# A table of due times in place of a seeded search, for a kernel whose order is packed ahead of the run

## The chip, the core and the metric

The kernel runs on one core of a Trainium2 chip. Its time is the device time of one launch in microseconds (us), the median of several runs. TensorE is called PE here, VectorE DVE, ScalarE ACT, GpSimd POOL, and the engine that issues the DMAs SP.

## What is computed

The program has two parts. The first is a linear attention with a delta rule: 4 batches of 8 heads, 768 steps, head width 48. The second is a gated layer over all 3072 tokens, with 384 features in, 1536 hidden and 384 out (called the expert layer or MoE here).

```python
k_n = k / (np.linalg.norm(k, axis=-1, keepdims=True) + 1e-06)
for t in range(S):
    kt, vt, bt = (k_n[:, :, t], v[:, :, t], beta[:, :, t, None])
    y[:, :, t] = np.einsum('bhd,bhde->bhe', q[:, :, t], state)
    v_old = np.einsum('bhde,bhd->bhe', state, kt)
    state = state + bt[:, :, :, None] * np.einsum('bhd,bhe->bhde', kt, vt - v_old)
...
a = x @ w_a
b = x @ w_b
return (a * b @ w_out).astype(np.float32)
```

Here `x` is the attention's output `y`, with the heads side by side.

## The kernel before, in words

**Tiling and stages.** The 768 steps are cut into 24 chunks of 32 steps, in six groups of four. For each group there is a stage `prep` (norms of the keys, products of keys and queries within a chunk, with 64 small products per chunk), a stage `solve` (a triangular system for each chunk, worked on DVE as a long chain of pairs of multiply into `tmp` and subtract from `b`), and a stage `steps` (for each chunk: products with the state `sh`, a difference `f`, a product with the solved factors `tt`, the update of the state `S_ps` from `u`, the output product with `at`, and then norm, transpose and split of y into two f16 halves `xb`). The small products of attention use 32- or 64-row tiles of the PE array; those of a chunk come as one operation, a group of 32 calls. In groups 2 to 5 POOL multiplies the values `vnb` with the norms; in groups 0 and 1 DVE does.

The expert layer works on pairs of chunks (256 tokens) and on 12 slices of 128 hidden features. For a pair and a slice there are two operations of 9 full products (`xb` by the weights `wh`, into a bank), then ACT scales one into `a`, DVE multiplies into `g`, ACT and DVE split `g` into the f16 halves `ghl`, and two operations of 3 products with `wo` add to the output. The stages `w0` to `w11` load, decode and scale one slice of weights each. The tile `late` holds several things in turn: weights as loaded, pieces of later chunks, and outputs.

**The order.** The kernel isn't issued in the order in which it is written. Each call on an engine is recorded as an operation of a `Plan` (`add`); calls inside `plan.group()` on one engine become one operation. There are 2937: 790 on PE, 1214 on DVE, 640 on ACT, 154 on POOL with its short copies, and the DMAs on SP. `link` finds the dependencies from the regions that are read and written. `pack` then runs through the work with a price for each operation, a list of those that are ready on each engine, and a due time `pri` for each: at each step an engine that is free takes its ready operation with the lowest due time, unless a rule holds it back (a bank of PSUM that isn't free, a `hold` time, small tiles that are preferred to full ones for a while after small ones, `JOIN`; an instruction fetch). The result is one sequence of operations, the bank that each uses (`bind`), and how many filler products of the tile `ones` PE gets ahead of an operation in the first part (`fill`). `issue` then emits the instructions in that sequence, and on the chip each engine takes its own instructions strictly in the order of emission, waiting on semaphores.

```python
while wait[e] and wait[e][0][0] <= t:
    i = heapq.heappop(wait[e])[1]
    heapq.heappush(can[e], (pri[i], i))
i = None
while can[e] and i is None:
    i = heapq.heappop(can[e])[1]
```

In the kernel before, `order` gets its due times in two steps. Fifteen passes of `pack`, forwards and backwards, set an operation's due time from how late it may end, less a fixed boost for its stream (`boost`), with the first loads ahead of everything. Then 30 fixed seeds each change some due times in `jitter`: 3% of the operations, or one stream, or 200 operations in a row, by random amounts. The last `pack` makes the sequence. All of this happens before the launch and isn't part of the measured time.

Of the kernel before, what the change touches and what calls it, by code (L numbers as in the profile page):

```python
# [40 lines left out]
def boost(o):  # L41
    return BOOST.get(o.stream + ("_pe" if o.stream == "moe" and o.eng == "PE" else ""), 0.0)
# [19 lines left out]
        self.rd, self.wr, self.deps, self.tag, self.banks = {}, {}, set(), "", set()  # L62


def jitter(pri, ops, seed):
    r = random.Random(seed)
    kind, amp = r.randrange(3), r.choice((500.0, 3000.0, 10000.0, 30000.0))
    names = sorted({o.stream for o in ops})
    name, start = r.choice(names), r.randrange(len(ops))
    move, new = r.gauss(0.0, amp), []  # L70
    for i, (o, p) in enumerate(zip(ops, pri)):
        u, g = r.random(), r.gauss(0.0, amp)
        if o.stream != "load":
            if kind == 0 and u < 0.03:
                p += g
            elif kind == 1 and o.stream == name:
                p += move
            elif kind == 2 and start <= i < start + 200:
                p += g
        new.append(p)  # L80
    return new


class Plan:
# [391 lines left out]
    HOLD = 300.0  # L476
    MARGIN = 5000.0
    WINDOW = 3413.0
    PASS = 15
    SEEDS = (500003, 500005, 500019, 500020, 500026, 500028, 500084, 500091, 500108, 500109, 500111, 500120, 500124, 500177, 500284, 500305, 500553, 500626, 500636, 500644, 500735, 500743, 500761, 500845, 500953, 501051, 501128, 501296, 501447, 501757)  # L480

    def order(self):


        self.link()
        ops = self.ops
        self.first = {o.eng: o for o in reversed(ops)}
        self.users = {}
        for o in ops:
            for b in o.banks:  # L490
                self.users[b] = self.users.get(b, 0) + 1
        self.succ = [[] for _ in ops]
        self.pred = [[] for _ in ops]
        for i, o in enumerate(ops):
            for j in o.deps:
                late = self.late(ops[j], o)
                self.succ[j].append((i, late))
                self.pred[i].append((j, late))
        pri = [o.pri - boost(o) - 1e12 * (o.stream == "load") for o in ops]
        for _ in range(self.PASS):  # L500
            found = self.pack(pri)
            stop = found[1] if found else [float(k) for k in range(len(ops))]
            _, stop, _, total, _ = self.pack([-t for t in stop], True)
            pri = [k - 1e12 if o.stream == "load" else total - t - boost(o) for k, (o, t) in enumerate(zip(ops, stop))]
        for seed in self.SEEDS:
            pri = jitter(pri, ops, seed)
        best = self.pack(pri)
        self.bind, self.fill = best[4]
        return best[2]

# [766 lines left out]
```

## Time and profile before

| what | value |
|---|---|
| runs | 632.46, 634.51, 637.12 us; median 634.51 |
| profiled execution | 633.64 us; its span from first to last instruction 631.9 us |
| PE busy | 608.3 us, 96% of the span |
| DVE, ACT, POOL busy | 435.6, 287.7, 56.5 us |
| granted PE clock, mean | 0.989 |
| moved by DMA | 42.85 MB |

How to read it: busy is the time in which an engine had an instruction under way, and since PE's instructions overlap, a busy PE isn't PE at its peak. A row of a group of instructions has the line of the code, engine, operation, output and inputs by the program's names, shape and count, then busy us, mean ns of one, the idle time of the engine just before them and what ended it. "issue" is time in which the engine waited for nothing that the profile shows. Since all instructions are emitted by `issue`, nearly all have one line, L532, and the filler has L523; tiles are told apart by name. A `bank` is a bank of PSUM, whatever it holds. Products of f32 show as two instructions each, so an operation of 32 small products shows as 64.

### The profile page before, as it was taken

The numbers are of one execution on the slowest core, as the hardware profiler recorded it, in microseconds if no ns is written. First come the engines' busy times: TensorE is split into PE (matmuls) and PEld (weight loads), VectorE is DVE, ScalarE is ACT, GpSimd is POOL, SyncE is SP. The second block draws the span as 40 slices with busy tenths as digits, with TensorE's granted clock in tenths as the row PEclk, the third lists the DMA queues.
The fourth block names the chain that finished last, engine by engine and source line by source line (L and its number), as shares of the span: only waits on it lengthen the run. The fifth ranks groups of instructions, "written<-read, shape, count | busy, mean of one in ns | idle before, by whom it ended". The sixth has DMA issues, their size and how long they took to land.

```text
span 631.9 us, 27357 instructions
## 1 busy us (share of the span) xinstructions
PE 608.3 (96%) x12228; PEld 476.9 (75%) x12228; DVE 435.6 (69%) x1215; ACT 287.7 (46%) x773; POOL 56.5 (9%) x158
## 2 busy tenths in 40 slices
PE   7989999999999998999999999999999999999997
PEld 6855767677778786777877787777878788787885
DVE  4977998889976789469965468875598544542222
ACT  2067863565843332544354334364423534542332
POOL 0221210110102102000020000020000000000000
PEclk8969999999999999999999999999999999999999
DMA  8554551352046510023200023100000000000000
GB/s 315 177 163 122 144 138 39 97 134 79 30 121 196 153 52 2 3 63 120 85 27 21 21 89 107 35 28 4 4 3 26 2 15 16 4 26 1 13 13 25
DMA packets 20756, 42.85 MB, mean 68 GB/s; under 512 B 2208, under 2 KB 5280, under 8 KB 20640
## 3 DMA queue, kind: packets, MB, share of 16 engines
q1 hardware_dynamic: 20640, 41.12, 21.7%
q8 instruction: 95, 1.56, 1.0%
q14 instruction: 21, 0.17, 0.1%
HBM read 36.39 MB, written 4.72 MB: 65 GB/s over the span
## 4 chain that ended last, share of the span: by engine, by line
PE 75%; DVE 11%; DMA 6%; issue 3%; ACT 3%; POOL 1%; SPq 0%; DVEq 0%; POOLq 0%; ACTq 0%
PE bank L532 73%; DMA late<-in_w 4%; PE S_ps L532 2%; DVE late L532 1%; DVE wh L532 1%; DVE b L532 1%; DVE g L532 1%; DMA rawb<-in_kqt 1%; DMA wh<-in_w 1%; DVE ghl L532 1%; DVE tmp L532 1%; DVE f L532 1%; DMA vnb<-in_vn 1%; DVE y L532 1%; POOL late L532 0%
## 5 line engine op out<-in xcount | busy, mean ns | idle before, releaser
L532 PEld LDWEIGHTS <-wh 128*128 128x128 f16 x2592 | 250.2, 98 | 46.4 <-issue 5.2
L532 PE MATMUL bank<-xb,wh 128*128 128x256 f16 x2160 | 257.5, 273 | 3.3 <-issue 2.0
L532 PE MATMUL bank<-wo,ghl 128*128 128x384 f16 x864 | 163.0, 326 | 1.8 <-issue 0.7
L532 ACT ACTIVATE a<-bank,part 128x256 f32<-128x256 f32 x144 | 68.0, 473 | 161.4 <-PE bank L532 159.9
L532 DVE TENSOR_TENSOR g<-bank,a 128x256 f32<-128x256 f32 x144 | 60.6, 422 | 84.7 <-ACT a L532 82.9
L532 PEld LDWEIGHTS <-ghl 128*128 128x128 f16 x864 | 81.4, 98 | 46.4 <-issue 1.9
L532 ACT CAST ghl<-g 128x256 f16<-128x256 f32 x144 | 58.0, 404 | 67.7 <-DVE g L532 50.5
L532 DVE TENSOR_TENSOR ghl<-g,ghl 128x256 f16<-128x256 f32 x144 | 61.0, 425 | 33.6 <-ACT ghl L532 30.2
L532 DVE TENSOR_TENSOR tmp<-b,b 128x31 f32<-128x31 f32 (+20 forms) x154 | 50.3, 327 | 3.1
L532 DVE TENSOR_TENSOR b<-b,tmp 128x31 f32<-128x31 f32 (+20 forms) x154 | 49.7, 322 | 3.5
L532 PE MATMUL bank<-late,wh 128*128 128x256 f16 x432 | 51.1, 273 | 0.0
L532 ACT ACTIVATE ys<-y 128x96 bf16<-128x96 f32 x96 | 26.1, 273 | 10.0 <-DVE y L532 9.7
L532 PE MATMUL bank<-rawb 48*32 48x64 f32 x1280 | 22.6, 220 | 7.0 <-POOL late L532 2.4
L532 PEld LDWEIGHTS bank<-rawb 48*32 48x32 f32 x1280 | 19.4, 108 | 10.6 <-POOL late L532 2.9
L532 POOL TENSOR_TENSOR z<-z,kb 128x4 f32<-128x4 f32 x24 | 9.6, 400 | 197.2 <-DVE z L532 181.6
L532 DVE TENSOR_TENSOR f<-vnb,bank 128x384 f32<-128x384 f32 x38 | 19.6, 548 | 8.7 <-PE bank L532 8.7
L532 ACT COPY sh<-S_ps 112x768 f32<-112x768 f32 x23 | 18.3, 796 | 14.6 <-PE S_ps L532 14.6
L532 PEld LDWEIGHTS bank<-sh,rawb 48*64 48x64 f32 x1216 | 19.9, 134 | 5.2 <-issue 2.1
L523 PE MATMUL bank<-ones 128*128 128x256 f32 x78 | 22.2, 450 | 1.1 <-DVE ones L532 1.1
L532 PE MATMUL bank<-sh,rawb 48*64 48x48 f32 x1216 | 22.5, 220 | 0.1
L532 PE MATMUL bank<-u,at 32*32 32x48 f32 x1536 | 21.5, 203 | 0.6 <-issue 0.6
L532 DVE SCALAR_TENSOR_TENSOR y<-bank,kb,y 128x384 f32<-128x384 f32 x23 | 14.2, 616 | 11.4 <-ACT y L532 10.4
(127 smaller groups left out, 640.8 us busy)
## 6 DMA issues: line engine op xcount, KB each, us to landing
late<-in_w SPq DMA_DIRECT2D x40, 288.0 KB, 3.2
rawb<-in_kqt SPq DMA_DIRECT2D x32, 256.0 KB, 2.7
out<-late SPq DMA_DIRECT2D x24, 192.0 KB, 1.9
vnb<-in_vn SPq DMA_DIRECT2D x10, 384.0 KB, 3.6
kb<-in_kn SPq DMA_DIRECT2D x9, 384.0 KB, 3.6
wh<-in_w SPq DMA_DIRECT2D x8, 288.0 KB, 3.3
rawb<-in_kqt SPq DMA_DIRECT2D x2, 1024.0 KB, 7.2
late<-in_kqt SPq DMA_DIRECT2D x8, 256.0 KB, 2.6
```

The source lines that it names most:

```text
L523: self.nc.tensor.matmul(self.pool[-1][0 : 32 + 96 * k, 0 : 32 + 224 * k], one, one.unsqueeze(1).broadcast_to([P, 1 + k, 32 + 96 * k])[:, 0 ...
L532: fn(*(self.place(a, lease) for a in args), **{k: self.place(a, lease) for k, a in kw.items()})
```

## The change

`jitter`, `PASS`, `SEEDS` and the passes are gone. In their place stands a table `DUE` of 2937 whole numbers, one for each operation in the order in which the program records them; ten times a number is the operation's due time, and `pack` runs once with these. Values near -99999999999 belong to the first loads. Operations, prices, holds, leases and `pack` itself are as before.

```diff
-import random
...
-def jitter(pri, ops, seed):
-    r = random.Random(seed)
-    kind, amp = r.randrange(3), r.choice((500.0, 3000.0, 10000.0, 30000.0))
...
+DUE = (
+    -12125,-8933,-13218,-100000000000,-100000000000,-100000000000,-99999999999,-99999999999,-99999999999,-99999999999,-99999999999,-99999999999,
...
+    49978,51481,60596,61726,60332,60386,52777,52323,52862,53125,61737,60175,64048,61278,58533,52510,52971,48928,60557,52767,52460,49435,
+)
...
-    PASS = 15
-    SEEDS = (500003, 500005, 500019, 500020, 500026, 500028, 500084, ...
...
-        pri = [o.pri - boost(o) - 1e12 * (o.stream == "load") for o in ops]
-        for _ in range(self.PASS):
-            found = self.pack(pri)
-            stop = found[1] if found else [float(k) for k in range(len(ops))]
-            _, stop, _, total, _ = self.pack([-t for t in stop], True)
-            pri = [k - 1e12 if o.stream == "load" else total - t - boost(o) for k, (o, t) in enumerate(zip(ops, stop))]
-        for seed in self.SEEDS:
-            pri = jitter(pri, ops, seed)
-        best = self.pack(pri)
+        best = self.pack([10.0 * p for p in DUE])
```

More of the change, by code (lines that the diff above doesn't have):

```diff
@@ L62, in __init__ @@
         self.rd, self.wr, self.deps, self.tag, self.banks = {}, {}, set(), "", set()
-def jitter(pri, ops, seed):
-    r = random.Random(seed)
-    kind, amp = r.randrange(3), r.choice((500.0, 3000.0, 10000.0, 30000.0))
[L68 to L81, printed above, removed]
+DUE = (
[117 rows of a table added]
+)
 class Plan:
@@ L478 @@
     WINDOW = 3413.0
-    PASS = 15
-    SEEDS = (500003, 500005, 500019, 500020, 500026, 500028, 500084, 500091, 500108, 500109, 500111, 500120, 500124, 500177, 500284, 500305, 500553, 500626, 500636, 500644, 500735, 500743, 500761, 500845, 500953, 501051, 501128, 501296, 501447, 501757)
     def order(self):
```

115 rows, old and new, of the table DUE are left out of this document.

## The prediction

> **What bounds the kernel now.** I read the page first, then the windows of all engines, PE's waits, the groups by shape, and last the timeline at three places.
>
> ```profile
> span 631.9 us, 27357 instructions
> PE 608.3 (96%) x12228; PEld 476.9 (75%) x12228; DVE 435.6 (69%) x1215; ACT 287.7 (46%) x773; POOL 56.5 (9%) x158
> PE 75%; DVE 11%; DMA 6%; issue 3%; ACT 3%; POOL 1%; SPq 0%; DVEq 0%; POOLq 0%; ACTq 0%
> ```
>
> PE is busy for 608.3 of 631.9 us and makes three quarters of the chain that ended last. An order of work can't make a product shorter. It can only remove what PE loses: idle time, filler products, and the loss at each change between small and full tiles. So I look for these three, by stage. In the next rows the columns are the stretch, then busy us and count for PE, weight load, DVE, ACT and POOL, then PE's granted clock.
>
> ```profile
> 0.00:20.00 20.00, 16.83 (x292) 13.66 (x293) 11.49 (x28) 4.89 (x9) 2.03 (x12) 0.91 0.83 284
> 20.00:40.00 20.00, 17.64 (x310) 13.06 (x308) 18.90 (x47) 5.39 (x18) 5.10 (x12) 0.85 0.57 165
> 40.00:60.00 20.00, 17.53 (x650) 11.97 (x650) 13.95 (x43) 15.21 (x45) 2.99 (x9) 0.89 0.51 140
> 100.00:120.00 20.00, 19.90 (x325) 14.29 (x326) 19.03 (x50) 8.77 (x25) 0.95 (x3) 1.00 0.09 23
> 240.00:260.00 20.00, 17.95 (x426) 14.04 (x424) 13.49 (x38) 7.75 (x17) 3.42 (x4) 1.00 0.01 2
> 580.00:600.00 20.00, 20.00 (x167) 16.06 (x165) 5.53 (x13) 6.23 (x14) 0.00 (x0) 1.00 0.03 11
> 0.00:60.00 60.00, 51.99 (x1249) 38.69 (x1250) 44.34 (x116) 25.49 (x71) 10.12 (x32) 0.89 0.64 196
> 60.00:500.00 440.00, 428.32 (x9325) 336.87 (x9326) 343.95 (x976) 213.06 (x573) 44.94 (x122) 1.00 0.23 67
> 500.00:560.00 60.00, 60.00 (x1109) 47.55 (x1107) 27.22 (x77) 26.77 (x80) 1.41 (x4) 1.00 0.03 9
> 620.00:640.00 20.00, 8.02 (x59) 5.50 (x57) 2.37 (x6) 3.23 (x7) 0.00 (x0) 0.94 0.06 20
> ```
>
> Idle PE time stands in three places: 60.00 - 51.99 = 8.0 us up to 60 us, 440.00 - 428.32 = 11.7 us from 60 to 500 us, and 11.9 - 8.02 = 3.9 us in the tail. From 500 to 620 us PE has no gap. The tail is the last scaling and the output transfer, which no order shortens.
>
> ```profile
> L532 PE MATMUL bank<-xb,wh 128*128 128x256 f16 x2160 | 257.5, 273 | 3.3 <-issue 2.0 <-DVE z L532 0.5 <-DVE at L532 0.4
> L532 PE MATMUL bank<-wo,ghl 128*128 128x384 f16 x864 | 163.0, 326 | 1.8 <-issue 0.7 <-ACT sh L532 0.6 <-DVE z L532 0.5
> L523 PE MATMUL bank<-ones 128*128 128x256 f32 x78 | 22.2, 450 | 1.1 <-DVE ones L532 1.1
> L532 PE MATMUL bank<-late,wh 128*128 128x256 f16 x432 | 51.1, 273 | 0.0
> 66.92 1.15 PE L532 MATMUL bank<-xb,wh 128*128 128x256 f16 x9
> ```
>
> The second loss is the filler: 22.2 us of products of `ones`, which compute nothing. The first product of the expert layer (the MoE part of the program) starts at 66.92 us. That layer has 2160 + 432 + 864 = 3456 products. In 580 to 600 us, with nothing else, 167 of them take 20.00 us, 0.1198 us each, so all need 414 us. From 66.92 to the start of the tail at 628.0 us there are 561.1 us; minus 414 and 11.7 of gaps leaves 135 us for the attention's small products, the late weights, and the third loss, the change of tile shape.
>
> ```profile
> 351.43 1.15 PE L532 MATMUL bank<-late,wh 128*128 128x256 f16 x9
> 352.51 0.88 PE L532 MATMUL bank<-f,tt 32*32 32x48 f32 x64
> 353.60 1.10 PE L532 MATMUL bank<-late 48*32 48x64 f32 x64 [0.21 <-DVE g L532]
> 354.63 0.93 PE L532 MATMUL S_ps<-u,kb 32*48 32x48 f32 x64
> 355.50 2.14 PE L532 MATMUL bank<-late,wh 128*128 128x256 f16 x18
> 357.47 1.14 PE L532 MATMUL bank<-wo,ghl 128*128 128x384 f16 x6
> ```
>
> A stretch of small tiles (352.51 to 355.50 here) stands between full ones, and such stretches come again for every chunk. From 66.92 us on about 21 of the 24 chunks have their five groups of small products still ahead, at about 1.0 us a group (the mean of the 0.88, 1.10 and 0.93 here, an estimate for all five): 105 us. With 10 to 15 us for the side products and the late weights that is 115 to 120 us, and 15 to 20 of the 135 us are lost at changes of shape; I use 18 us.
>
> **The change part by part.** It removes `jitter`, the 15 passes and the 30 seeds, and gives each of the 2937 operations its own due time. Instructions, tiles, prices, holds and leases stay. It adds no wait by itself: the packing still starts the ready operation with the lowest due time and keeps every dependency. What moves is the place of an operation in its engine's queue. I compared the two lists of due times by rank alone. On PE half of the 790 operations move by at most 4 places, a tenth by more than 16. On DVE half of the 1214 move by more than 28. The largest shift by stage is in the DVE work of the triangular solves of groups 4 and 5, whose middle operations are due 97 and 127 places earlier. The 24 first loads keep their sequence up to one v load, two places earlier on SP; later weight and piece loads change by up to 8 places, in a queue whose DMA share is 0.03 to 0.23 after 60 us. I cost these DMAs at nothing; bounds from the DMA waits below are 1.8 us either way. What is left are three terms.
>
> ```profile
> PE bank L532 <- issue: 5.5, 10, 0.7
> PE bank L532 <- POOL late L532: 2.4, 2, 1.4
> PE bank L532 <- DMA rawb<-in_kqt: 1.8, 1, 1.8
> PE bank L532 <- POOL vnb L532: 1.6, 1, 1.6
> PE bank L532 <- DVE b L532: 1.2, 1, 1.2
> PE bank L532 <- ACT ys L532: 1.1, 1, 1.1
> PE bank L532 <- DVE zi L532: 1.1, 2, 0.7
> PE bank L532 <- DVE z L532: 1.1, 2, 0.5
> ```
>
> *Term 1, up to 66.92 us.* The chain is the load of the pieces, the solve of group 0 on DVE, the first two chunks, then the first product. DVE is 18.90 of 20 us busy in 20 to 40 us, so a cheaper place for it is scarce; in 40 to 60 us it is 13.95 busy and PE waits 1.1 us for ys and 1.1 us for zi. These 2.2 us are pure order: short operations queued behind weight decoding. Filler and gaps together (22.2 + 8.0 us) bound the gain, but before 30 us they cover DMA and the solve. I take -2.0 us, bounds -8.0 (all gaps) and +3.0 (the waits for ys, zi and b once more, 3.4 us, rounded down).
>
> *Term 2, gaps from 60 to 500 us.* Of 11.7 us the waits for operations that stand late in another queue are POOL late 2.4, POOL vnb 1.6, DVE z 1.1 and four smaller ones of ACT sh, ACT u, DVE at and DVE g of 1.4 together: 6.5 us. Most of the rest is issue time (5.5 us over the whole span), which a new order moves and doesn't remove. The two solves that come due earlier are also the ones that make later chunks, and so PE work, available. I take two thirds of 6.5, -4.5 us; bounds -10 and +6 (the 6.5 us of waits once more).
>
> *Term 3, changes of shape.* With the PE operations sorted by due time alone, small tiles stand in 91 stretches in the old list and 83 in the new one; the order that was issued has 85. 18 us over 85 is 0.21 us each, so 8 fewer are -1.7 us; bounds -5 (a quarter of 18, rounded) and +1.7.
>
> The sum: -2.0 - 4.5 - 1.7 = -8.2 us. The profiled execution took 633.64 us (its span 631.9 and 1.7 around it), so 625.4 us; the median of the runs, 634.51, is 0.9 higher, so 626.3. I say 626, which is 1.3% faster. About 1%, 6.3 us, is what a measurement of this kernel can tell from no change.
>
> One cover can go: the granted clock.
>
> ```profile
> 34.00:42.00 8.00, 7.29 (x231) 0.51 0.55 152
> ```
>
> In the rows above the clock is 0.91, 0.85 and 0.89 up to 60 us, and 1.00 after; inside, from 34 to 42 us, it is 0.51. If the lower state is one half, that is 2 x (0.09 + 0.15 + 0.11) x 20 = 14 us at half speed, mostly under filler and waits, worth at most 7 us. The longest wait of PE in the table is 1.8 us, and the clock stayed at 1.00 through all later ones, so I put no price on it. [...]
>
> **The rivals.**
>
> *Nothing to measure, 632 us.* The gaps change places. For it: in 100 to 120 us DVE is busy for 19.03 of 20 us and PE for 19.90, so what is moved forward on DVE there delays something else; the issue waits stay; only term 1 and a part of term 3 hold, together 2 to 3 us. It also covers the case that the table hardly does what it says, since dependencies, holds and bank leases may force nearly the old order. Against it: 6.5 us of gaps wait for an operation and not for an engine's capacity, and half of DVE's queue moves.
>
> *Slower, 641 us: the solves run beside POOL's products.* The place is the end of the solve of group 2, before's largest gap after 60 us:
>
> ```profile
> 238.37 0.40 DVE L532 TENSOR_TENSOR tmp<-b,b 128x231 f32<-128x231 f32 x1
> 238.57 3.90 POOL L532 TENSOR_TENSOR vnb<-vnb,nm 128x384 f32<-128x384 f32 x4 [16.53 <-DVE nm L532]
> 238.69 0.82 DVE L532 TENSOR_TENSOR s<-nm 128x32 f32<-128x32 f32 x1
> 241.83 0.86 DVE L532 TENSOR_TENSOR tmp<-b,b 128x207 f32<-128x207 f32 x1
> 243.13 1.10 PE L532 MATMUL bank<-rawb 48*32 48x64 f32 x64 [1.61 <-POOL vnb L532]
> 245.14 0.33 DVE L532 TENSOR_TENSOR tmp<-b,b 128x175 f32<-128x175 f32 x1
> ```
>
> While POOL multiplies, a DVE step takes 0.86 us for 207 elements, where 231 took 0.40 just before: each such step loses up to 0.46 us, and behind it wait the evictions that free PE's banks. PE lost 20.00 - 17.95 = 2.05 us in this window. Before has this meeting with such a loss once. If solves meet the v products of the three other groups of this kind too (the four groups after the first two use POOL for them), PE loses 3 x 2.05 = 6.2 us, at most 3 x 3.90 = 11.7 us when DVE stands still for all of POOL's time. With none of the gains that is 633.6 + 6.2 = 639.8, up to 645.3; I name 641. It decides when, in three groups, DVE's spare time in the 20 us around the meeting falls below the 3.90 us of POOL. Against it: in the latter half DVE has such time (13.49 busy of 20 here), and a solve with a due time earlier by 100 places may also come clear of the products. [...]
>
> *Much faster, 613 us.* Term 1 reaches its bound of -8.0, term 2 -8 and term 3 -4: 633.6 - 20 = 613.6. For it: filler and gaps of the start hold 30 us. Against it: DVE's 18.90 of 20 us there, and the loads.
>
> **How the numbers follow.** The forecast (616 to 628) has 0.46, much faster (under 616) 0.09, nothing to measure (628 to 638) 0.37, slower (over 638) 0.08. The line for faster by over 1% is 634.5 - 6.3 = 628.2, nearly the forecast's upper edge; I count 0.54 as faster, leaving 0.38 within 1% and 0.08 slower. The terms' bounds added up give 610.6 and 644; not all of them fall on one side at once. The range of 8 in 10 takes the forecast, the upper part of "nothing to measure" and a little of the third rival: 614 to 637.
>
> **What would show it.** Term 1: the first MoE product starts before 66.92 us, at about 65. Term 2: PE's idle time from 60 to 500 us is about 7 us instead of 11.7, without the two waits on POOL. Term 3: fewer stretches of small tiles, about 78. The tail stays near 3.9 us and PE has no gap from 500 us on. [...]

## The result, and the profile after

The changed kernel takes 629.44 us (median; 627.59 to 630.36), against 635.30 us (632.46 to 637.12) for the kernel before, each in 7 runs. The ratio is 0.9919, with a 95% interval from 0.9898 to 0.9940. So the table makes the kernel faster by 0.8%, 3.8 to 6.5 us, where 8.2 us were forecast. Of all runs below, one of 646.36 us lies over 1.5% above the fastest run of its kernel, and it is left out of that kernel's median. The profiled execution took 629.44 us, its span 627.7 us, 4.2 us shorter than before.

From the page of the changed kernel, the same lines as before and the line of the loads of instructions, which comes up again below:

```profile
span 627.7 us, 27362 instructions
...
PE 607.3 (97%) x12228; PEld 476.6 (76%) x12228; DVE 434.2 (69%) x1215; ACT 286.7 (46%) x773; POOL 57.1 (9%) x158
...
q8 instruction: 95, 1.56, 1.0%
```

The windows of the changed kernel (stretch, then busy us and count of PE, weight load, DVE, ACT, POOL, then PE's clock):

```profile
0.00:60.00 60.00, 51.34 (x1218) 38.78 (x1221) 44.16 (x116) 24.43 (x67) 8.63 (x32) 0.86 0.62 194
60.00:500.00 440.00, 431.78 (x9397) 339.50 (x9390) 342.75 (x977) 214.27 (x586) 46.59 (x122) 1.00 0.22 67
500.00:560.00 60.00, 60.00 (x1108) 47.43 (x1107) 27.61 (x76) 26.45 (x73) 1.86 (x4) 1.00 0.04 14
...
620.00:640.00 20.00, 4.17 (x26) 2.29 (x24) 1.38 (x4) 1.97 (x4) 0.00 (x0) 0.94 0.05 20
```

PE's idle time from 60 to 500 us fell from 11.7 to 440.00 - 431.78 = 8.2 us. Up to 60 us it rose a little, from 8.0 to 8.7 us. The tail is 7.7 - 4.17 = 3.5 us, before 3.9. Together the idle time is 3.2 us less, and PE's busy time is 1.0 us less (607.3 after 608.3): that is the 4.2 us.

PE's waits in the changed kernel (us in total, times, longest):

```profile
PE bank L623 <- issue: 4.6, 8, 1.1
PE bank L623 <- DVE g L623: 2.5, 5, 1.0
PE bank L623 <- DMA rawb<-in_kqt: 2.3, 1, 2.3
...
PE bank L623 <- ACT wh L623: 1.3, 1, 1.3
PE bank L623 <- DVE zi L623: 1.3, 2, 0.7
...
PE bank L623 <- DVE z L623: 1.0, 2, 0.5
```

The two rows on POOL, `late` with 2.4 us and `vnb` with 1.6 us before, are gone. In their place stand five waits on `g`, 2.5 us, where before had this row:

```profile
PE bank L532 <- DVE g L532: 0.2, 1, 0.2
```

How the wait on `vnb` went is seen in the timeline of the changed kernel, where the multiplications of group 3's values now come ahead of the group's first products:

```profile
223.84 1.78 POOL L623 TENSOR_TENSOR vnb<-vnb,nm 128x384 f32<-128x384 f32 x2 [4.53 <-DVE nm L623]
223.91 1.03 DVE L623 TENSOR_TENSOR tmp<-b,b 128x231 f32<-128x231 f32 x1
...
228.97 1.79 POOL L623 TENSOR_TENSOR vnb<-vnb,nm 128x384 f32<-128x384 f32 x2 [3.23 <-DMA vnb<-in_vn]
229.12 0.96 DVE L623 TENSOR_TENSOR tmp<-b,b 128x252 f32<-128x252 f32 x1
...
230.12 0.93 DVE L623 TENSOR_TENSOR b<-b,tmp 128x252 f32<-128x252 f32 x1
...
231.08 0.42 DVE L623 TENSOR_TENSOR tmp<-b,b 128x255 f32<-128x255 f32 x1
...
232.35 1.62 PE L623 MATMUL bank<-wo,ghl 128*128 128x384 f16 x9 [1.02 <-DVE g L623]
```

POOL's four multiplications still meet the solve on DVE, now in two pairs, 15 and 10 us earlier than the four in a row of before. One step beside the first pair takes 1.03 us, two beside the second 0.96 and 0.93 us, the next one 0.42. Behind the second pair `g` is late and PE waits 1.02 us, where it had lost 2.05 us between 240 and 260 us before.

The first product of the expert layer starts at 67.30 us, not earlier than the 66.92 of before:

```profile
67.30 0.93 PE L623 MATMUL bank<-xb,wh 128*128 128x256 f16 x7
```

### The profile page after: what moved, and what is told of

Same layout as the page of the kernel before. It is cut to its first block, busy times and chain, and to the rows that moved or that the text cites. A ratio compares the mean times of both kernels' runs of the same rounds, so it can differ in the third digit from the quotient of the medians.

```text
span 627.7 us, 27362 instructions
## 1 busy us (share of the span) xinstructions
PE 607.3 (97%) x12228; PEld 476.6 (76%) x12228; DVE 434.2 (69%) x1215; ACT 286.7 (46%) x773; POOL 57.1 (9%) x158
## 3 DMA queue, kind: packets, MB, share of 16 engines
q8 instruction: 95, 1.56, 1.0%
## 4 chain that ended last, share of the span: by engine, by line
PE 72%; DVE 11%; DMA 7%; issue 4%; ACT 3%; POOL 1%; SPq 0%; DVEq 0%; POOLq 0%; ACTq 0%
PE bank L623 70%; DMA late<-in_w 5%; PE S_ps L623 2%; DVE b L623 2%; DVE g L623 1%; DVE tmp L623 1%; DMA wh<-in_w 1%; DMA rawb<-in_kqt 1%; DVE ghl L623 1%; DVE wh L623 1%; DVE late L623 1%; POOL vnb L623 1%; DVE f L623 1%; DMA vnb<-in_vn 1%; ACT a L623 1%
```

## The experiments

My theory after the result was that the gain is made of PE waits removed one by one after 60 us. The rivals were that the start carries it; that a removed wait comes back later; and that it is a matter of where PE's instructions stand in their stream, since eight to ten waits ("issue") have no releaser in the profile.

For the experiments a kernel gets a finished sequence, the bank of every lease and the filler, in place of the table:

```diff
-        best = self.pack([10.0 * p for p in DUE])
-        self.bind, self.fill = best[4]
-        return best[2]
+        self.bind, self.fill = dict(enumerate(BIND)), FILL
+        return list(SEQ)
```

A mixture of two sequences takes the operations of one up to a point, and then all others in the other's order. Where a lease's bank is taken there, it gets another that is free. That touched 0 to 6 leases of 345 in the mixtures at one cut, and 11 and 27 in the two with an inserted stretch. Each run stands beside runs of the kernel before on the same chip, 633.7 to 634.8 us in the median.

### The start alone, and the rest alone

```diff
-SEQ = new
+SEQ = new up to 62 us, then old          (e1_new_start)
+SEQ = old up to 62 us, then new          (e2_old_start)
```

> The new sequence for what is planned up to 62 us, then the old one for the rest. Theory (the gain is waits of PE removed after 60 us): no gain, 0 to +0.6 us on before, so about 635 us where before is 635. Rival (the gain is in the start): 629 to 630 us.

> The old sequence for what is planned up to 62 us, then the new one for the rest. Theory: the whole gain of the change, 628.5 to 629.5 us where before is 635. Rival (the start): 634 to 635 us.

Measured: with the new start 634.20 us, ratio 0.9990 (0.9963 to 1.0018), no gain. With the old start and the new rest 629.22 us, ratio 0.9913 (0.9880 to 0.9946), the whole gain. The rival of the start falls, though the first interval leaves room for a part of up to 2.3 us.

### How the gain adds up

```diff
+SEQ = new up to 180 us, then old         (e3_new_to_180)
+SEQ = new up to 345 us, then old         (e9_new_to_345)
```

> The new sequence up to 180 us, then the old one. Theory (waits removed one by one along the span; the new kernel is 1.5 us ahead at the eighth chunk's norm): 1.5 us less than before, 633.5 where before is 635. Rival (all comes from the two waits on POOL at 243 and 327 us): as before, 635. Rival (start and the stage where DVE is full, 60 to 180 us, carry it): 630.

> The new sequence up to 345 us, then the old one. Theory (the gain adds up along the span from removed waits): about two thirds of the gain of 5 to 6 us, 630.5 to 632 where before is 634.5. Rival (the gain needs the whole of the new sequence, and a mixture loses it): as before, 634.5. Rival (all of it is won by 345 us): 629.

Measured: 633.57 us, ratio 0.9973 (0.9953 to 0.9993), then 630.53 us, ratio 0.9940 (0.9908 to 0.9973). After 180 us a third of the gain is there, after 345 us about three quarters. Both medians are what the theory said. The second interval doesn't exclude that all of the gain is won by 345 us, and neither run says which kind of loss shrinks.

### One stretch at a time

```diff
+SEQ = old, but the operations planned for 200 to 262 us in the new order   (e7_old_but_200_262)
+SEQ = old, but the operations planned for 300 to 345 us in the new order   (e8_old_but_300_345)
```

> The old sequence, with the operations of the stretch planned for 200 to 262 us put into the new sequence's order (58 places of PE and 107 of DVE differ; group 3's norms come earlier). Theory (a removed wait of PE is worth its length): the wait of 1.6 us on POOL and the 0.45 us behind it at 243 us go, a wait of about 1 us on g comes, as in after; 1 to 2 us less than before, 633.5. Rival (a removed gap comes back later, since the next chunk isn't earlier): as before, 635, with the idle time moved into the next 100 us.

> The old sequence, with the operations of the stretch planned for 300 to 345 us in the new order (32 places of PE, 64 of DVE). Theory: the wait of 1.35 us on POOL late at 327.6 us shrinks to 0.4 us as in after; about 1 us less than before, 634. Rival: as before, 635, with the time lost elsewhere.

Measured: 634.27 us, ratio 0.9994 (0.9970 to 1.0019), and 633.89 us, ratio 0.9996 (0.9968 to 1.0024). Neither gains a microsecond that can be told. In the first, the waits aimed at did change. Its waits of PE:

```profile
PE bank L591 <- issue: 8.3, 11, 1.4
...
PE bank L591 <- POOL late L591: 1.3, 1, 1.3
PE bank L591 <- DVE g L591: 1.2, 2, 1.0
...
PE bank L591 <- POOL vnb L591: 0.4, 1, 0.4
```

The wait on POOL vnb shrank from 1.6 to 0.4 us and one on g came, as in the changed kernel. But the issue waits grew from 5.5 to 8.3 us. In the second, the wait of 1.35 us on POOL at 327 us went, and at the same product an issue wait of 1.16 us stood in its place:

```profile
327.98 1.10 PE L591 MATMUL bank<-rawb 48*32 48x64 f32 x64 [1.16 <-issue]
```

A stretch's gain of 1 to 2 us is within the interval of these runs, so its size stays open. What the two traces show is that the issue waits aren't a fixed background: they move with the order, by as much as the waits on engines do.

### Where the instructions stand in PE's stream

`pack` itself counts PE's instructions. Its `fetch` takes them in blocks of 256, from a start of 63 (`BEGIN`), prices the load of each block and holds an operation back whose block would not have come; after 60 us it does the same for counts 14 lower and 14 higher (`SHIFTS`). So each order is built for its own place, and the shifts that follow are all larger than what it allows for.

The next runs leave the sequence alone and change the filler ahead of it, so that all later instructions of PE stand some places later or earlier.

```diff
-FILL = {60: [0, 7], 72: [0, 3], 122: [0, 28], 248: [0, 1]}
+FILL = {60: [0, 7], 72: [0, 3], 122: (64, 20), 248: [0, 1]}    (e4_after_shift, 96 later)
+FILL = {60: (32, 7), 72: [0, 3], 122: [0, 28], 248: [0, 1]}    (e5_after_shift64 and e6_before_shift64, 64 later)
```

The numbers are counts of small and large filler products ahead of an operation. A later variant puts one product of 512 columns in place of two of 256:

```diff
-FILL = {... 122: [0, 28] ...}
+FILL = {... 122: (0, 0, 14) ...}      (e10_after_wide14 and e11_before_wide14, 56 earlier)
+FILL = {... 122: (0, 14, 7) ...}      (e12_after_wide7, 28 earlier)
```

> The new sequence, but in the third stretch of filler 8 large products give way to 64 small ones, so 96 more instructions stand ahead of everything that follows on PE at nearly the same time. Theory (the gain is in the order): as after, within 1 us, 629 to 630.5. Rival (the gain is where PE's instruction stalls fall by chance, the issue waits): up to 3 us slower, 631 to 633, with other issue waits and more of them.

> The new sequence with all its filler, and 32 small products (64 instructions) more in the gap of 2.3 us ahead of PE's first real products, where PE waits for a DMA anyway; all that follows stands 64 instructions later in PE's stream. Theory A (the gain is in the order, and the place of the instructions in PE's stream matters little): 629 to 630 where before is 635. Rival B (the order is fitted to the places at which PE's instructions arrive): more issue waits than the 4.6 us of after, 2 to 5 us slower than after, 631 to 635.

> The same 32 small products ahead of the old sequence. Theory A: as before, 634 to 636. Rival B: if the old order is fitted as well, slower by as much as the run with the new order, 637 to 640; if the old one isn't fitted and the new one is, as before, and then the gain is that fit.

> The new sequence, with 14 filler products of double width in place of the 28 of the third stretch: same busy time on PE, 56 instructions fewer ahead of all the rest. Theory B (the order is fitted to the places at which PE's instructions arrive): slower than after by 3 to 8 us, 632 to 638, with more issue waits after 60 us. Theory A (the loss of the run with 64 instructions more came from the start alone): as after, 628.5 to 630.5.

> The same double-width filler ahead of the old sequence. Theory B: slower than before, 637 to 643, and slower than the same shift on the new order by 2 to 6 us, if the new order keeps a gain of its own at any place. Theory A: as before, 634.5. If it comes out equal to the new order with the same shift, the gain of the change is fit to the places and nothing else.

> The new sequence, with 7 double-width products in place of 14 of the third stretch: 28 instructions fewer. Theory B: between after and the run with 56 fewer, 630 to 634. Theory A: as after, 628.5 to 630.5.

Measured, each ratio against the kernel before on the same chip, and span, PE's idle time from 60 to 500 us and all its issue waits from one profiled execution of each:

| places | order | median us | ratio to before (95%) | span us | idle, 60 to 500 | issue waits |
|---|---|---|---|---|---|---|
| 96 later | new | 637.98 | 1.0057 (1.0028 to 1.0085) | 640.1 | 14.5 | 9.1 |
| 64 later | new | 639.84 | 1.0088 (1.0057 to 1.0120) | 638.1 | 13.5 | 9.8 |
| 64 later | old | 644.14 | 1.0146 (1.0103 to 1.0189) | 641.1 | 15.8 | 11.1 |
| as built | new | 629.44 | 0.9919 (0.9898 to 0.9940) | 627.7 | 8.2 | 4.6 |
| as built | old | 635.30 | 1 | 631.9 | 11.7 | 5.5 |
| 28 earlier | new | 628.33 | 0.9921 (0.9889 to 0.9953) | 626.1 | 7.6 | 3.2 |
| 56 earlier | new | 629.19 | 0.9933 (0.9907 to 0.9959) | 625.7 | 7.4 | 4.7 |
| 56 earlier | old | 630.47 | 0.9956 (0.9928 to 0.9984) | 627.5 | 7.8 | 2.1 |

The run with 96 later is clouded: its clock in the first 60 us was 0.74 (0.86 in the changed kernel) and 0.973 in the mean (0.986), with small products in the place of large ones, its first expert product came at 74.50 us, and its profiled execution took 641.83 us, well above the median. The others keep all the large filler or its busy time: with 56 earlier and the old order its third stretch runs from 16.56 to 28.85 us, before from 16.56 to 28.91 us.

More instructions cost more than either expectation had. Fewer cost nothing with the new order, where the theory of a fitted order expected 3 to 8 us for 56, and they made the old order faster, which neither theory expected. Being outside of what `pack` allows for is therefore not enough to explain a loss.

Sixty-four instructions cost some 10 us with either order, twice the effect of the change. The issue waits double, and the small groups are cut in pieces by them. In the run with the old order 64 later:

```profile
124.66 0.37 PE L591 MATMUL bank<-b,tt 32*32 32x16 f32 x20 [1.29 <-issue]
...
276.41 0.38 PE L591 MATMUL S_ps<-u,kb 32*48 32x48 f32 x12 [1.43 <-issue]
...
364.72 0.31 PE L591 MATMUL S_ps<-u,kb 32*48 32x48 f32 x9 [1.19 <-issue]
```

Not all of the 10 us are such waits after 60 us: the first expert product came at 69.81 us with the new order and at 69.01 with the old, 2.5 and 2.1 us later, and PE's busy time grew too (612.5 us with the old order, after 608.3), for a reason that no run isolates.

What are these waits? The line of queue q8 says that 95 loads brought 1.56 MB of instructions, 16,384 bytes each by the DMA records. PE has 24,456 matmuls and weight loads. If these loads are its stream, that is 95 x 16,384 / 24,456 = 63.6 bytes for each, and a load holds some 257 of them. I take 256, the number by which `pack` counts: an estimate, which the places below bear out. I set the end of every issue wait against the end of the last such load in the trace's DMA records:

```
kernel                 issue waits   from the end of a load to the end of the wait
before                 10            1.30 to 1.54 us in all 10
after                  8             1.25 to 1.46 us in 7, 6.1 us in one
old order, 64 later    18            1.24 to 1.50 us in 17, 3.4 us in one
new order, 64 later    14            1.21 to 1.60 us in 13, 11.5 us in one
old order, 56 earlier  5             1.30 to 1.53 us in all 5
```

A load comes every 6.7 us on average (631.9 / 95), so by chance some 6% of the waits would end 1.2 to 1.6 us after one. The place in the stream leaves little room for chance. With PE's matmuls and weight loads of the trace counted in blocks of 256, the waits that follow a load all stand at one place of the block: 191 at the start of each run, close to the 256 - 63 = 193 at which `pack` lets the first block end, then falling slowly in order of time to about 150 at 430 to 440 us and 139 at 535 us. The three that don't follow a load stand at 115, 247 and 179, and the waits on other engines anywhere from 1 to 251. From this I take it that PE was waiting for the next block of instructions. Why the place falls isn't shown; instructions of PE that the profile doesn't count would do it. Many of these waits cut a group of small products in two. There, 64 matmuls and their 64 weight loads take 0.9 us, so a load of 256 lasts only 1.8 us there.

The most telling run is the old order 56 places earlier. Its two rows on POOL are those of before, and all its waits with a named releaser come to 12.5 us, after 12.8 before; its issue waits are 2.1 us in place of 5.5 (1.8 of them ahead of products into a bank, 0.3 into `S_ps`):

```profile
PE bank L592 <- POOL late L592: 2.4, 2, 1.3
...
PE bank L592 <- issue: 1.8, 4, 0.9
PE bank L592 <- POOL vnb L592: 1.6, 1, 1.6
```

With no operation moved its span is 4.4 us shorter, and by its ratio of 0.9956 it gains 2.8 us, about half of what the change does. Of the 4.4 us 0.8 us came at the start, where its first expert product stood at 66.11 us:

```profile
66.11 1.15 PE L592 MATMUL bank<-xb,wh 128*128 128x256 f16 x9
```

What follows for the change: at three places the new order has the lower median, by 5.9 us as built (5.1 by the ratio), 4.3 us with 64 later and 1.3 us with 56 earlier (4.2, 3.0 and 1.8 us in span). As built the gain is clear; with 64 later the two intervals overlap a little, and with 56 earlier over most of their length, so there the orders can't be told apart by time. The traces show in what they differ: from 60 to 500 us PE's waits with a named releaser are 6.6, 7.0 and 6.2 us with the old order (as built, 64 later, 56 earlier) and 3.9, 5.7 and 5.2 us with the new one, in one execution of each. So the order has a gain of its own there, of 1.0 to 2.7 us, and part of the measured gain comes with the place at which the old order was built, which isn't its best. At the best place tried for each, 628.33 us stands against 630.47 us with overlapping intervals; the old order with 28 fewer instructions wasn't run. How much each part is can't be told closer than this.

No version beats the changed kernel clearly. The one with 28 fewer instructions has the lowest median, 628.33 us, and its ratio of 0.9921 is that of the changed kernel.

## Why the prediction was right, and where it was off

**Direction and mechanism.** PE was the bound, busy for 96% of the span before and 97% after, and PE's losses are what shrank. The time lies in the stated range, and 629.4 us is 3.4 us above the forecast of 626. But the range of 614 to 637 also holds the time of before, so lying in it says little. The measured time is above the forecast's own band of 616 to 628 and within 1% of before, the case that had the second-best chance; what sets it apart from that case is that the gain is clear of noise. That the sum came this close is in part luck: 56 instructions fewer ahead of the old order, of which the prediction knows nothing, would have taken about half of the gain away.

**Term 1, the start, -2.0 us: wrong.** The new start alone gives a ratio of 0.9990, whose interval just reaches 2.3 us of gain, the old start with the new rest has the whole gain, and the first expert product isn't earlier. I had counted PE's waits for ys and zi as pure order. After the change a wait on ACT of 1.3 us stands at the product that had waited 1.1 us for ys, and the zi wait is 1.3 us. I take it that the chain through DMA, solve and DVE sets the start, whatever PE waits for by name; no run isolates that.

**Term 2, the gaps, -4.5 us: right in kind, -3.5 us measured.** (Two thirds of 6.5 us are 4.3, not 4.5.) The two rows on POOL went as forecast, 4.0 us. I left out what replaces them: 2.3 us more on g. In place of the 6.5 us counted there, 3.9 us of waits with a named releaser stand from 60 to 500 us. That issue time "moves and isn't removed" nearly held for the change itself, 3.9 us from 60 to 500 us before and 3.7 after; as a rule it was wrong, since the experiments moved all of it between 2.1 and 11.1 us.

**Term 3, changes of shape, -1.7 us: too large.** The sequence that was issued has 83 stretches of small tiles, against 85, not 78. At 0.21 us each, my estimate from what was left of 135 us, that is 0.4 us; PE's busy time fell by 1.0 us in all. The trace of before has such a loss from 67 us on: the first small product starts 0.20 us after the last full one, and the first full one 0.14 us after the last small one (medians of 76 changes each), where full ones start 0.11 us apart and small ones 0.01. Those are 0.09 + 0.13 = 0.22 us more for a stretch, close to the estimate.

**The step behind terms 2 and 3 that failed** is the reading of the table by rank. I took the rank of a due time as the place in the queue: 97 and 127 places earlier for the solves of groups 4 and 5, and a median of 28 places on DVE. In the two sequences as issued, half of the 1215 DVE operations moved by at most one place, and the solves of groups 4 and 5 by 1 and 2 places in the median. On PE 474 of 790 operations stand elsewhere, half of all by at most one place and a tenth by 5 or more. A due time decides only among operations that are ready at the same moment; where one is ready at a time, its number can be nearly anything. The change is a smaller one than its table looks. That its gain was smaller for this reason isn't shown.

**The rivals.** The slower case needed more meetings of the solve with POOL's products. The meeting at group 3 stayed and got cheaper, 1.02 us of PE in place of 2.05. The case without a gain was nearer than I put it: term 1 was nothing and part of term 2 came back on another engine. The third rival needed a shorter start, and there was none. A rival was missing altogether: that the time depends on the place of the instructions. I had the row, 5.5 us of issue waits in 10 places, and the code of `fetch`, and priced it as a constant.

## What to carry to other kernels

A list of due times isn't an order: before pricing a change of such a table, compare the sequences that come out, engine by engine. Waits that a profile can't name deserve a look of their own; where they end a fixed time after a load of instructions (1.2 to 1.6 us here), a few more or fewer instructions ahead of them are a cheap experiment: here 56 fewer made the old order 3 to 4 us faster and 64 more made both orders some 10 us slower, where the change itself is worth 5 to 6 us. And an effect of one percent from a new order should be measured at more than one such place before it is put down to the order.

## What the runs showed of the hardware

In this kernel PE's waits without a releaser go with the loads of instructions in q8. Waits of 0.15 to 1.8 us ended 1.2 to 1.6 us after a load of 16,384 bytes in 52 of 55 cases, at one slowly falling place of a block of 256, and 64 more instructions ahead of the work cost 10 us of 635, about half of it in such waits. Of the 95 loads of before 85 are followed by no such wait; the other 10 are, with 5.5 us of waits, and 64 instructions more made that 11.1 us.

A step of the solve on DVE (`tmp` from `b`, or `b` from `b` and `tmp`) with no multiplication of POOL beside it took at most 0.43 us in the changed kernel (298 steps) and at most 0.44 us in the kernel before (297 steps). Beside the multiplications of `vnb` three steps of five took 1.03, 0.96 and 0.93 us in the changed kernel, and two of five 0.86 and 0.74 us before. Not every step is slowed: in the kernel before, one of 231 elements took 0.39 us at 239.43 us, while POOL's multiplications went on. No run isolates why a step is slowed.
